# Attention and feed-forward in one kernel: the bias rows of the last eight groups stored in two steps, q, k and v loaded whole, bias read with fewer transfers

## Chip, cores and metric

One core of one Trainium2 chip. The metric is the device time of one execution in microseconds (us); three runs of the kernel before gave 684.4 us in the median (683.91 to 684.7).

## What is computed

Attention over q, k, v of shape (4 batches, 8 heads, 576 positions, 64), with an additive bias that a small network makes from the two positions, then a feed-forward layer over the 2304 tokens. Cut from the reference:

```python
scores = scale * np.matmul(q, k.transpose(0, 1, 3, 2))
pos = np.arange(S)
rel = (pos[:, None] - pos[None, :]).astype(np.float32)
psi_rel = np.log1p(np.abs(rel))
psi_i = np.log1p(np.maximum(pos[:, None].astype(np.float32), 1.0))
x = (psi_rel / psi_i)[..., None]
h = np.maximum(x @ w1 + b1, 0.0)
bias = h @ w2
scores = scores + bias.transpose(2, 0, 1)[None, :, :, :]
...
x = np.ascontiguousarray(attn_out.transpose(0, 2, 1, 3)).reshape(B * S, H * D)
h = x @ w_in
g = np.maximum(0.01 * h, h)
return (g @ w_out).astype(np.float32)
```

The bias depends on head and positions alone, so it is made once (8 x 576 x 576 numbers) and used for all four batches.

## The kernel before

**Bias generation.** The 576 query rows are made in 36 row groups of 16, in the order of the list GEN (line 35). A group has 16 rows by 8 heads, so it fills 128 partitions. Groups are counted here from 0 to 35 by their place in that order. For each, VectorE (DVE) and ScalarE (ACT) make the hidden layer (`gen_r`, line 115), TensorE (PE) contracts it (`gen_mm`, line 128), and ACT evicts the result into an SBUF buffer (`gen_ev`, line 139); the second part of the last three evictions is DVE's. SyncE (SP) then stores the group to one of five DRAM tensors (line 158): groups 2 to 9 make tensor 0, 10 to 17 tensor 1, 20 to 27 tensor 2, 28 to 35 tensor 3, and groups 0, 1, 18, 19 tensor M. The store also turns the relative layout into rows.

**Attention.** There are 16 units, a unit being one pair of heads in one batch; the pair changes every fourth unit. A unit has nine score tiles, in the order A0, B0, A1, B1, M, A2, B2, A3, B3 (A and B are the two heads, the number is the block of 128 queries, M holds the last 64 queries of both heads). `step(n)` (line 365) handles tile n = 9 u + i: q k^T on PE into one of two buffers `ps_s` (`qk_mm`), then on DVE the sum with the bias and the row minimum (`softmax_a`, line 277), the transposes of tile n-3 on PE, the product with v (`pv`, line 344), and the exponential on ACT. Tiles with number 0, 1, 2, 3 and M read the bias loaded from the tensor of that name. `load_bias` (line 171) loads a head pair from such a tensor: three transfers for a numbered one, two for M. Its calls during generation are in `gen_tick` (line 167); the later pairs are loaded during units 3, 7 and 11.

**Unit inputs.** `load_unit` (line 187) loads q and k of a unit twice, once to partitions 0 to 63 and once to 64 to 127, in four transfers; `load_v` (line 195) loads v in one transfer of 512 columns and two small ones (the last 64 keys, padded with zeros that DVE writes at the start). From unit 1 on, q and k are split into a rounded part (DVE, lines 207 and 212) and a rest (GpSimd, lines 219 and 222).

**Order.** All of this is written out by hand: each engine runs its instructions in the order of the code. SP issues all DMAs, in one queue, in that order. Each DMA is given one of eight semaphores in turn; before one is issued, the DMA that held the same semaphore eight places earlier must have landed (waits named DMAHW0 to DMAHW7 below). A load of bias also waits for the stores of its tensor. During unit 0 the code runs all of the generation first (line 37), then step 0. After the attention comes the feed-forward part, which the change doesn't touch.

Of the kernel before, what the change touches and what calls it, by code (L numbers as in the profile page):

```python
# [8 lines left out]
F32 = mybir.dt.float32  # L9
# [25 lines left out]
GEN = [16, 17] + list(range(16)) + [34, 35] + list(range(18, 26)) + list(range(33, 25, -1))  # L35
# [4 lines left out]


@with_exitstack
def attention_ffn(ctx: ExitStack, tc: tile.TileContext, qt, kt, vm, vt, wi, wo, cst, out):
    nc = tc.nc
    PS = bass.MemoryType.PSUM
    xp = ctx.enter_context(tc.tile_pool(name="xp", bufs=1))
# [16 lines left out]
    raw_b = [[ap.tile([128, c], F32, name=f"raw{c}{i}") for c in (2 * S, KW)] for i in range(2)]  # L63
    ident = ap.tile([128, 128], F32, name="ident")
    make_identity(nc, ident[:])
    vt_b = [ap.tile([128, 2, 64], F32, name=f"vt{i}") for i in range(3)]
    for t in vt_b:
        nc.vector.memset(t[0:64, 1, :], 0.0)
        nc.vector.memset(t[64:128, 0, :], 0.0)
# [4 lines left out]
    raw_0 = [gp.tile([128, c], F32, name=f"raw{c}") for c in (2 * S, KW)]  # L74
# [4 lines left out]
    e_b = [gp.tile([128, W], F32, name=f"e{i}")[:] for i in range(7)]  # L79
# [18 lines left out]
    gr, gps = {}, {}  # L98

    def gen_w(T):  # L100
        return max(S - 16 * T, 16 * T + 16)
# [2 lines left out]
    for T in GEN:  # L104
# [4 lines left out]
        for _ in range(4):  # L109
            e = min(cost, key=lambda c: load[c] + cost[c])  # L110
# [28 lines left out]
    def gen_ev(T):  # L139
        pt, o0 = gps.pop(T)  # L140
        R, F = 16 * T + 15, S - 16 * T
        e = e_b[GEN.index(T) % len(e_b)]
        nc.scalar.activation(out=e[:, R:W], in_=pt[:, o0:o0 + F], func=AF.Copy, scale=ips[:, T:T + 1])  # L143
        if GEN.index(T) < 33:
            nc.scalar.activation(out=e[:, 0:R], in_=pt[:, o0 + R:o0:-1], func=AF.Copy, scale=ips[:, T:T + 1])
        else:
            nc.vector.tensor_scalar(out=e[:, 0:R], in0=pt[:, o0 + R:o0:-1], scalar1=ips[:, T:T + 1], scalar2=None, op0=ALU.mult)
        if T < 16:
            c, r0 = str(T // 8), 16 * (T % 8)
        elif T < 18:  # L150
            c, r0 = "M", 16 * (T - 16)
        elif T < 34:
            c, r0 = str(2 + (T - 18) // 8), 16 * ((T - 18) % 8)
        else:
            c, r0 = "M", 32 + 16 * (T - 34)
        a = r0 * H * PIT + 1
        dst = scr[c][a:a + 16 * (H * PIT + 1)].rearrange("(i x) -> i x", i=16)[:, 0:H * PIT].rearrange("i (h p) -> i h p", h=H)[:, :, 0:W]
        nc.sync.dma_start(out=dst, in_=e)

    def gen_tick(g):  # L160
        if g + 1 < 36:
            gen_r(g + 1)
# [24 lines left out]
    def load_unit(u):  # L187
        hp, b = divmod(u, B)
        q_, k_ = raw_b[u % 2] if u else raw_0
# [3 lines left out]
        raw[u] = (q_, k_)  # L193

    def load_v(u):
        hp, b = divmod(u, B)
        v_ = ap.tile([128, 4, 128], F32, tag="v", name="v", bufs=3)
        nc.sync.dma_start(out=v_[:], in_=vm[hp, b])
        for h in range(2):
            nc.sync.dma_start(out=vt_b[u % 3][64 * h:64 * h + 64, h, :], in_=vt[hp, b, h])  # L200
        vv[u] = v_

    def split_hi(u, what):
        q_, k_ = raw[u]
        if what == "q":
            qs = qs_b[u % 2]
            nc.vector.tensor_copy(qs[:].rearrange("p (a c) -> p a c", a=2), q_[:].rearrange("p (a c) -> p a c", a=2)[:, :, 64:S])  # L207
            ks1 = ap.tile([128, KW], F32R, tag="ks1", name="ks1", bufs=2)
            ks2 = ap.tile([128, KW], F32R, tag="ks2", name="ks2", bufs=2)
            qk[u] = (qs, ks1, ks2)  # L210
        else:
            nc.vector.tensor_copy(qk[u][1][:], k_[:])

    def split_lo(u, what, a):
        q_, k_ = raw[u]
# [128 lines left out]
    def pv():  # L344
        _, u, g = pv_q.pop(0)
        hp, b = divmod(u, B)
        o, pt = outs.pop((u, g)), PT[:, g]
        if (u, g) == (HP * B - 1, 1):
            o = pstile("s")
        for jb in range(5):  # L350
            for h in range(2):
                if jb < 4:
                    l, r = vv[u][:, jb, 64 * h:64 * h + 64], pt[:, 2 * jb + h, :]
                else:
                    l, r = vt_b[u % 3][:, h, :], pt[:, 8, :]
# [233 lines left out]
    with tc.manual_schedule():  # L589
# [6 lines left out]
        for n in range(NTILE + LAG + 6):  # L596
            u, i = divmod(n, 9)
# [55 lines left out]
        pt = pv_out[0][3]  # L653
# [185 lines left out]
```

## Time and profile before

| | us |
|---|---|
| median of 3 runs | 684.4 |
| the profiled execution | 685.03 |
| its span, first to last instruction | 683.3 |
| PE busy | 675.2 |
| DVE busy | 492.1 |
| ACT busy | 407.9 |
| POOL busy | 205.8 |

The span is divided into bias generation (to about 49 us), unit 0 (to about 60 us), the other units (to about 302 us) and the feed-forward part. PE is busy in nearly all of it; DVE and ACT are busiest at the start. Engine names: PE TensorE, PEld its weight loads, DVE VectorE, ACT ScalarE, POOL GpSimd, SP SyncE with its DMA queue.

### The profile page before, as it was taken

What the parts mean: (1) busy time and instruction counts of PE and PEld (TensorE: products, weight loads), DVE (VectorE), ACT (ScalarE), POOL (GpSimd) and SP (SyncE); (2) the same over time, 40 slices, a digit from 0 to 9 for tenths busy, and PEclk for the clock granted to TensorE, in tenths of its full rate; (3) what the DMA queues carried; (4) which work ended last, traced back from release to release, by engine and by line L of the source; (5) the groups of instructions that cost most, each with busy time, mean ns of one, the idle gap of its engine ahead of it and who ended that gap; (6) DMA issues with size and microseconds to landing.
All of it is one profiled execution on the core that took longest, in us unless ns stands there. A gap on an engine that the chain in (4) does not pass through costs nothing.

```text
span 683.3 us, 11911 instructions
## 1 busy us (share of the span) xinstructions
PE 675.2 (99%) x4254; PEld 551.8 (81%) x4254; DVE 492.1 (72%) x1083; ACT 407.9 (60%) x883; POOL 205.8 (30%) x227
## 2 busy tenths in 40 slices
PE   9999999999999999999999999999999999999997
PEld 5436778887778777787889898898989898988986
DVE  8997789999999998589999868534343754343342
ACT  8987777888878888685555455333333543333332
POOL 0004445666666654420000503111114512111110
PEclk9999999999999999999999999999999999999999
DMA  9997679669955976135267336532333345332302
GB/s 213 350 324 201 194 219 248 175 199 269 282 166 164 307 226 197 55 114 202 94 200 244 141 94 230 195 115 108 107 108 108 122 173 196 141 109 108 108 1 92
DMA packets 39931, 117.85 MB, mean 172 GB/s; under 512 B 9024, under 2 KB 13760, under 8 KB 37440
## 3 DMA queue, kind: packets, MB, share of 16 engines
q1 hardware_dynamic: 39728, 116.96, 54.2%
q8 instruction: 33, 0.54, 0.3%
q14 instruction: 26, 0.21, 0.1%
q10 hardware_dynamic: 144, 0.13, 0.1%
HBM read 86.78 MB, written 30.29 MB: 171 GB/s over the span
## 4 chain that ended last, share of the span: by engine, by line
PE 91%; DVE 3%; ACT 2%; DMA 2%; issue 1%; POOL 0%; DVEq 0%; SPq 0%; POOLq 0%; ACTq 0%
PE ps_t L522 24%; PE ps_s L563 19%; PE ps_o L356 12%; PE ps_s L254 10%; PE ps_o L563 10%; PE ps_t L319 9%; DVE r L125 2%; PE ps_s L239 1%; PE ps_o L308 1%; PE ps_o L337 1%; DMA w1a<-w 1%; DMA bias<-scr 1%; PE ps_t L136 1%; PE ps_o L136 1%; ACT x L143 1%
## 5 line engine op out<-in xcount | busy, mean ns | idle before, releaser
L534 DVE TENSOR_TENSOR c<-ps_t,c 128x384 f32<-128x384 f32 x164 | 88.9, 555 | 130.5 <-PE ps_t L522 129.4
L541 ACT ACTIVATE g<-c 128x384 fp32r<-128x384 f32 x96 | 50.4, 525 | 181.1 <-DVE c L534 157.0
L563 PE MATMUL ps_s<-ws,g 128*128 128x512 f32 x576 | 148.3, 393 | 0.0
L563 PEld LDWEIGHTS ps_s<-ws,g 128*128 128x128 f32 x576 | 106.7, 188 | 16.9
L277 DVE CUSTOM_DVE_ANT_0 p<-ps_s,bias 128x576 f32<-128x576 f32 x128 | 95.4, 752 | 20.6 <-PE ps_s L254 18.1
L285 ACT ACTIVATE p<-p,mx 128x576 f32<-128x576 f32 x128 | 99.9, 780 | 9.0 <-DVE mx L277 6.7
L522 PE MATMUL ps_t<-xo,w1c 128*128 128x384 f32 x504 | 99.8, 336 | 0.8 <-DVE c L534 0.6
L472 POOL TENSOR_TENSOR ws<-y,ws 128x512 fp32r<-128x512 f32 x32 | 42.7, 1334 | 184.2 <-PE ps_t L522 147.4
L335 ACT COPY PT<-ps_t 128x512 f32<-128x512 f32 x128 | 73.8, 577 | 40.0 <-PE ps_t L319 40.0
L522 PEld LDWEIGHTS ps_t<-xo,w1c 128*128 128x128 f32 x504 | 89.3, 188 | 8.8 <-DVE c L534 2.3
L254 PE MATMUL ps_s<-ks,qs 128*128 128x288 f32 x480 | 93.7, 317 | 0.0
L522 PE MATMUL ps_t<-xo,w1a 128*128 128x384 f32 x474 | 93.2, 335 | 0.0
L522 PEld LDWEIGHTS ps_t<-xo,w1a 128*128 128x128 f32 x474 | 84.4, 188 | 5.9
L254 PEld LDWEIGHTS ps_s<-ks,qs 128*128 128x128 f32 x480 | 67.6, 189 | 13.3 <-issue 4.8
L319 PE MATMUL ps_t<-ident,p 128*128 128x128 f32 x512 | 77.5, 274 | 0.0
L563 PE MATMUL ps_o<-ws,g 128*128 128x512 f32 x288 | 74.0, 393 | 0.0
L546 DVE TENSOR_TENSOR g<-gf,g 128x384 fp32r<-128x384 f32 x96 | 61.1, 637 | 14.5 <-ACT gf L542 14.4
L319 PEld LDWEIGHTS ps_t<-ident,p 128*128 128x128 f32 x512 | 61.0, 140 | 9.1 <-issue 8.2
L356 PE MATMUL ps_o<-PT,v 128*64 128x288 f32 x496 | 67.0, 412 | 0.0
L219 POOL TENSOR_TENSOR qs<-raw,qs 64x512 fp32r<-64x512 f32 x30 | 37.8, 1279 | 75.0 <-DVE qs L207 73.4
L563 PEld LDWEIGHTS ps_o<-ws,g 128*128 128x128 f32 x288 | 53.4, 188 | 8.5
L356 PEld LDWEIGHTS ps_o<-PT,v 128*64 128x64 f32 x496 | 32.9, 136 | 23.6 <-issue 2.7
(131 smaller groups left out, 913.7 us busy)
## 6 DMA issues: line engine op xcount, KB each, us to landing
w1a<-w SPq DMA_DIRECT2D x10, 1792.0 KB, 7.7
w1c<-w SPq DMA_DIRECT2D x9, 1792.0 KB, 7.5
raw<-kt SPq DMA_DIRECT2D x32, 304.0 KB, 6.0
raw<-qt SPq DMA_DIRECT2D x32, 288.0 KB, 4.5
w<-w1a SPq DMA_DIRECT2D x20, 448.0 KB, 5.5
raw<-wi SPq DMA_DIRECT2D x16, 512.0 KB, 3.8
raw<-wo SPq DMA_DIRECT2D x16, 512.0 KB, 4.7
scr<-x SPq DMA_DIRECT2D x21, 295.5 KB, 5.2
```

The lines of the kernel that those rows point to most:

```text
L254: nc.tensor.matmul(s_[:, S0 + HS * hh:S0 + HS * hh + HS], qs[:, c0:c0 + 128], ks[:, k0 + HS * hh:k0 + HS * hh + HS], start=(j == 0), stop= ...
L277: nc.vector.tensor_tensor_reduce(out=p, in0=s_[:, S0:S0 + S], in1=bt, scale=-0.125, scalar=3.4e38, op0=ALU.add, op1=ALU.min, accum_out=i)
L285: nc.scalar.activation(out=p, in_=p, func=AF.Exp, bias=i, scale=-1.0, accum_out=sm)
L319: nc.tensor.transpose(t0[:, 128 * jb:128 * jb + 128], p[:, p0 + 128 * jb:p0 + 128 * jb + 128], ident[:])
L335: nc.scalar.copy(out=PT[:, g, 0:8, c].rearrange("p (j h) c -> p j h c", h=2)[:, :, h, :], in_=t0[:].rearrange("p (j c) -> p j c", j=4))
L356: nc.tensor.matmul(o[64 * h:64 * h + 64, 0:HS], l, r, start=(jb == 0), stop=(jb == 4))
L472: eng.tensor_sub(t[:, 1], y2[c % MF][:], t[:, 0].bitcast(F32))
L522: nc.tensor.matmul(o, w[:, a, PROD[j], c], x[:, b, k, :], start=(n == 0), stop=(n == 5))
L534: nc.vector.tensor_add(a if c == src else c_new(g, c), bank[g, j], a)
L541: nc.scalar.activation(out=t[:, 0], in_=h, func=AF.Prelu, alpha=0.01)
L546: nc.vector.tensor_sub(t[:, 1], gf.pop((g, c))[:], t[:, 0].bitcast(F32))
L563: nc.tensor.matmul(o, t[:, a, c], w[:, b], start=(m == 0 and n == 0), stop=(m == NG - 1 and n == 5))
```

## The change

- Groups 28 to 35 (tensor 3) are stored in two steps. During generation only the rows of the first two heads are stored, in one transfer per head (16 rows of 591 numbers). The whole rows of all eight heads are stored during unit 0, one group in each of the steps 5 to 12.
- The buffers of the evictions are taken two places further on, so that those of the last eight groups lie in the tiles `x1`, which stay free until unit 4.
- The bias of tensor 2 is loaded at tick 34 of the generation instead of tick 37. Loads of a numbered tensor are two transfers (128 x 2 x 512 and 128 x 2 x 64), that of M is one: 128 rows, taken from DRAM with the two heads as the outer dimension and 64 rows within each.
- q and k of a unit, both copies, come in one transfer of 128 x 2368 numbers, and v with its padded last block in one of 128 x 640. The host lays them out so. The six memsets of DVE are gone.

The core of the diff:

```diff
@@ gen_ev
-        e = e_b[GEN.index(T) % len(e_b)]
+        e = e_b[(GEN.index(T) + 2) % len(e_b)]
...
-        nc.sync.dma_start(out=dst, in_=e)
+        if GEN.index(T) < 36 - LATE:
+            nc.sync.dma_start(out=dst, in_=e)
+        else:
+            for h in range(2):
+                nc.sync.dma_start(out=dst[:, h], in_=e[h::H])
+            late.append((dst, e))
@@ gen_tick
-        for c in {16: "0", 24: "1", 27: "M", 37: "23"}.get(g, ()):
+        for c in {16: "0", 24: "1", 27: "M", 34: "2", 37: "3"}.get(g, ()):
@@ load_bias
-            nc.sync.dma_start(out=t[0:64, :], in_=rows[:, 2 * hp, :])
-            nc.sync.dma_start(out=t[64:128, :], in_=rows[:, 2 * hp + 1, :])
+            nc.sync.dma_start(out=t[:], in_=rows[:, 2 * hp:2 * hp + 2, :].rearrange("i h p -> h i p"))
...
-            nc.sync.dma_start(out=t[:, 0, :], in_=rows[:, 2 * hp, :])
-            nc.sync.dma_start(out=t[:, 1, 64:S], in_=rows[:, 2 * hp + 1, 0:512])
-            nc.sync.dma_start(out=t[:, 1, 0:64], in_=rows[:, 2 * hp + 1, 512:S])
+            f, two = t[:].rearrange("p h c -> p (h c)"), rows[:, 2 * hp:2 * hp + 2, :]
+            main = bass.AP(f.tensor, f.offset, [f.ap[0], [640, 2], [1, 512]])
+            nc.sync.dma_start(out=main, in_=two[:, :, 0:512])
+            nc.sync.dma_start(out=f[:, 512:640].rearrange("p (h c) -> p h c", h=2), in_=two[:, :, 512:S])
@@ load_unit
-        for t, src in ((q_, qt), (k_, kt)):
-            for p in (0, 64):
-                nc.sync.dma_start(out=t[p:p + 64], in_=src[hp, b])
+        nc.sync.dma_start(out=t[:], in_=qk_in[hp, b])
@@ load_v
-        v_ = ap.tile([128, 4, 128], F32, tag="v", name="v", bufs=3)
-        nc.sync.dma_start(out=v_[:], in_=vm[hp, b])
-        for h in range(2):
-            nc.sync.dma_start(out=vt_b[u % 3][64 * h:64 * h + 64, h, :], in_=vt[hp, b, h])
+        v_ = ap.tile([128, 5, 128], F32, tag="v", name="v", bufs=3)
+        nc.sync.dma_start(out=v_[:], in_=v_in[hp, b])
@@ step
+            if 5 <= n < 5 + LATE:
+                dst, e = late[n - 5]
+                nc.sync.dma_start(out=dst, in_=e)
```

SP's queue before, from the load of M to the loads of tensors 2 and 3 (scr_81 is tensor 2, scr_82 tensor 3; x_69 and x_70 hold evicted groups; a DMA row's shape is its destination's):

```order
L176 DMA biasM<-scrM 64x576 [waits DMAHW1_49]
L177 DMA biasM<-scrM 64x576 [waits DMAHW2_49]
L158 DMA scr_81<-x_69 16x8x591 [waits DMAHW3_49,Activation_49]
L158 DMA scr_82<-x_69 16x8x591 [waits DMAHW4_49,Activation_49]
...
L158 DMA scr_82<-x_70 16x8x591 [waits DMAHW3_49,DVE_49]
L180 DMA bias<-scr_81 128x576 [waits DMAHW4_49]
L181 DMA bias<-scr_81 128x512 [waits DMAHW5_49]
L182 DMA bias<-scr_81 128x64 [waits DMAHW6_49]
L180 DMA bias<-scr_82 128x576 [waits DMAHW3_49,DMAHW2_49,DMAHW7_49,DMAHW1_49,DMAHW0_49]
```

The same place in the change, from the load of M to the second DMA of group 31, which is the ninth behind it:

```order
L178 DMA biasM<-scrM 128x1x576 [waits DMAHW5_49]
L156 DMA scr_81<-x_69 16x8x591 [waits DMAHW6_49,Activation_49]
L159 DMA scr_82<-x_69 16x591 [waits DMAHW7_49,Activation_49]
L159 DMA scr_82<-x_69 16x591 [waits DMAHW0_49]
L159 DMA scr_82<-x_69 16x591 [waits DMAHW1_49,Activation_49]
L159 DMA scr_82<-x_69 16x591 [waits DMAHW2_49]
L159 DMA scr_82<-x_70 16x591 [waits DMAHW3_49,Activation_49]
L159 DMA scr_82<-x_70 16x591 [waits DMAHW4_49]
L159 DMA scr_82<-x_70 16x591 [waits DMAHW5_49,Activation_49]
L159 DMA scr_82<-x_70 16x591 [waits DMAHW6_49]
```

The load of M is one row where there were two, and the first DMA of group 31 waits for the semaphore that this load holds (DMAHW5). Behind these rows, to the late stores, the queue reads in the change:

```order
L159 DMA scr_82<-x_70 16x591 [waits DMAHW1_49,DVE_49]
L159 DMA scr_82<-x_70 16x591 [waits DMAHW2_49]
L183 DMA bias<-scr_81 128x2x512 [waits DMAHW3_49]
L184 DMA bias<-scr_81 128x2x64 [waits DMAHW4_49]
L159 DMA scr_82<-x_70 16x591 [waits DMAHW5_49,DVE_49]
...
L183 DMA bias<-scr_82 128x2x512 [waits DMAHW5_49,DMAHW6_49,DMAHW2_49,DMAHW7_49,DMAHW1_49,DMAHW0_49]
L184 DMA bias<-scr_82 128x2x64
L192 DMA raw_84<-qk_in 128x2368 [waits DMAHW3_49]
L367 DMA scr_82<-x_69 16x8x591 [waits DMAHW4_49,DMAHW2_49,DMAHW1_49]
```

The loads from tensor 2 stand four stores further ahead than before (behind group 33 instead of 35), those from tensor 3 still stand behind the last store of that tensor, and the whole-row stores stand behind the q and k of unit 2.

## Rows read from the trace of the kernel before

**Rows 1.** The page's first part: busy time, share of the span, instructions.

```profile
PE 675.2 (99%) x4254; PEld 551.8 (81%) x4254; DVE 492.1 (72%) x1083; ACT 407.9 (60%) x883; POOL 205.8 (30%) x227
```

**Rows 2.** Chain that ended last, 0 to 66 us: start us, us, what.

```profile
50.91 4.77 DMA bias<-scr
...
55.81 0.76 DVE p L277
...
56.63 0.76 PE ps_s L248 x4
...
60.90 2.58 PE ps_o L356 x20
```

**Rows 3.** Windows of 2 us: PE, PEld, DVE, ACT, POOL busy, PEclk, DMA share, GB/s.

```profile
6.00:8.00 2.00, 2.00 (x28) 1.11 (x21) 1.86 (x5) 1.51 (x4) 0.00 (x0) 1.00 1.01 237
22.00:24.00 2.00, 2.00 (x19) 0.89 (x15) 2.00 (x8) 2.00 (x7) 0.00 (x0) 1.00 1.04 377
54.00:56.00 2.00, 1.53 (x11) 0.83 (x9) 0.23 (x2) 1.27 (x4) 0.00 (x0) 1.00 0.60 214
56.00:58.00 2.00, 1.37 (x9) 0.83 (x10) 1.57 (x6) 1.39 (x4) 0.98 (x4) 1.00 0.89 269
```

**Rows 4.** Timeline of DVE, 55 to 80 us: start us, us, what, [idle before <-releaser].

```profile
55.81 0.76 DVE L277 CUSTOM_DVE_ANT_0 p<-ps_s,bias 128x576 f32<-128x576 f32 x1 [1.77 <-DMA bias<-scr]
...
58.03 0.76 DVE L277 CUSTOM_DVE_ANT_0 p<-ps_s,bias 128x576 f32<-128x576 f32 x1 [0.43 <-PE ps_t L319]
...
59.33 0.69 DVE L309 COPY PT<-ps_o 128x512 f32<-128x512 f32 x1
...
65.30 0.68 DVE L207 CAST qs<-raw 128x1024 fp32r<-128x1024 f32 x1
```

**Rows 5.** Timeline of PE, 46 to 64 us.

```profile
55.26 0.27 PE L337 MATMUL ps_o<-ident,p 128*128 128x128 f32 x1
56.63 0.76 PE L248 MATMUL ps_s<-raw,raw 64*128 64x288 f32 x4 [1.10 <-DVE mx L277]
...
59.57 0.78 PE L254 MATMUL ps_s<-ks,qs 128*128 128x288 f32 x4
...
60.83 2.16 PE L356 MATMUL ps_o<-PT,v 128*64 128x288 f32 x16
```

**Rows 6.** Timeline of SP's DMA issues, 0 to 62 us.

```profile
13.52 1.23 SPq L158 DMA_DIRECT2D scrM<-e  x2
...
40.96 0.52 SPq L158 DMA_DIRECT2D scr<-x  x1
41.54 0.64 SPq L176 DMA_DIRECT2D biasM<-scrM  x1
...
43.37 7.49 SPq L158 DMA_DIRECT2D scr<-x  x9
50.91 0.70 SPq L180 DMA_DIRECT2D bias<-scr  x1
...
55.17 0.32 SPq L180 DMA_DIRECT2D bias<-scr  x1
55.53 0.43 SPq L181 DMA_DIRECT2D bias<-scr  x1
```

**Rows 7.** Timeline, ends of the evictions of groups 0, 26, 31 and 35.

```profile
7.24 0.48 ACT L145 ACTIVATE e<-ps_t,cs 128x271 f32<-128x271 f32 x1
...
37.82 0.69 ACT L145 ACTIVATE x<-ps_t,cs 128x399 f32<-128x399 f32 x1
...
43.43 0.84 ACT L145 ACTIVATE x<-ps_t,cs 128x495 f32<-128x495 f32 x1
...
48.11 0.67 DVE L147 TENSOR_SCALAR x<-ps_t,cs 128x431 f32<-128x431 f32 x1 [0.23 <-ACT x L143]
```

**Rows 8.** Stores `scr<-x` to 62 us: count, issue ns min/median/max, first and last start.

```profile
L158 SPq DMA_DIRECT2D scr<-x x21: 523/764/1173, 19.5 to 50.0; - x21
```

**Rows 9.** Tile `bias` to 62 us: from issue to landing, its twelve transfers.

```profile
DMA to landing us min/median/max: 2.7/4.4/5.9
```

**Rows 10.** DMA issues: count, KB of each, median us from issue to landing.

```profile
out<-x SPq DMA_DIRECT2D x1, 128.0 KB, 1.9
```

More of the change, by code (lines that the diff above doesn't have):

```diff
@@ L27 @@
 RAWS = 3
+LATE = 8
 PRE = 3
@@ L42, in attention_ffn @@
 @with_exitstack
-def attention_ffn(ctx: ExitStack, tc: tile.TileContext, qt, kt, vm, vt, wi, wo, cst, out):
+def attention_ffn(ctx: ExitStack, tc: tile.TileContext, qk_in, v_in, wi, wo, cst, out):
     nc = tc.nc
@@ L61, in pstile @@
         return ps.tile(shape, F32, tag=tag, name="ps_" + tag)
-    raw_b = [[ap.tile([128, c], F32, name=f"raw{c}{i}") for c in (2 * S, KW)] for i in range(2)]
+    raw_b = [ap.tile([128, 2 * S + KW], F32, name=f"raw{i}") for i in range(2)]
     ident = ap.tile([128, 128], F32, name="ident")
     make_identity(nc, ident[:])
[L66 to L69, printed above, removed]
     qs_b = [ap.tile([128, 1024], F32R, name=f"qs{i}") for i in range(2)]
     PT = ap.tile([128, 2, 10, HS], F32, name="PT")
-    raw_0 = [gp.tile([128, c], F32, name=f"raw{c}") for c in (2 * S, KW)]
+    raw_0 = gp.tile([128, 2 * S + KW], F32, name="raw")
     cs = gp.tile([128, S + 214], F32, name="cs")
@@ L96, in gen_setup @@
         nc.gpsimd.tensor_scalar(out=w2d, in0=w2d, scalar1=8.0, scalar2=None, op0=ALU.mult)
-    gr, gps = {}, {}
+    gr, gps, late = {}, {}, []
     def gen_w(T):
@@ L188, in load_unit @@
         hp, b = divmod(u, B)
-        q_, k_ = raw_b[u % 2] if u else raw_0
-        for t, src in ((q_, qt), (k_, kt)):
-            for p in (0, 64):
-                nc.sync.dma_start(out=t[p:p + 64], in_=src[hp, b])
-        raw[u] = (q_, k_)
+        t = raw_b[u % 2] if u else raw_0
+        nc.sync.dma_start(out=t[:], in_=qk_in[hp, b])
+        raw[u] = (t[:, 0:2 * S], t[:, 2 * S:2 * S + KW])
     def load_v(u):
         hp, b = divmod(u, B)
-        v_ = ap.tile([128, 4, 128], F32, tag="v", name="v", bufs=3)
-        nc.sync.dma_start(out=v_[:], in_=vm[hp, b])
-        for h in range(2):
-            nc.sync.dma_start(out=vt_b[u % 3][64 * h:64 * h + 64, h, :], in_=vt[hp, b, h])
+        v_ = ap.tile([128, 5, 128], F32, tag="v", name="v", bufs=3)
+        nc.sync.dma_start(out=v_[:], in_=v_in[hp, b])
         vv[u] = v_
@@ L206, in split_hi @@
             qs = qs_b[u % 2]
-            nc.vector.tensor_copy(qs[:].rearrange("p (a c) -> p a c", a=2), q_[:].rearrange("p (a c) -> p a c", a=2)[:, :, 64:S])
+            nc.vector.tensor_copy(qs[:].rearrange("p (a c) -> p a c", a=2), q_.rearrange("p (a c) -> p a c", a=2)[:, :, 64:S])
             ks1 = ap.tile([128, KW], F32R, tag="ks1", name="ks1", bufs=2)
@@ L211, in split_hi @@
         else:
-            nc.vector.tensor_copy(qk[u][1][:], k_[:])
+            nc.vector.tensor_copy(qk[u][1][:], k_)
     def split_lo(u, what, a):
@@ L351, in pv @@
             for h in range(2):
[L352 to L355, printed above, removed]
+                l, r = vv[u][:, jb, 64 * h:64 * h + 64], pt[:, 2 * jb + h if jb < 4 else 8, :]
                 nc.tensor.matmul(o[64 * h:64 * h + 64, 0:HS], l, r, start=(jb == 0), stop=(jb == 4))
@@ L810 @@
     kd = np.concatenate([kd[0::2], kd[1::2, :, :, 512:], kd[1::2]], -1)
+    qkd = np.concatenate([qd.reshape(HP, B, D, 2 * S), kd], -1)
+    qkd = np.concatenate([qkd, qkd], 2)
     vd = v.transpose(1, 0, 2, 3).reshape(HP, 2, B, S, D).transpose(0, 2, 3, 1, 4).reshape(HP, B, S, 2 * D)
     vm = vd[:, :, :512].reshape(HP, B, 4, 128, 128).transpose(0, 1, 3, 2, 4)
-    vt = vd[:, :, 512:].reshape(HP, B, 64, 2, D).transpose(0, 1, 3, 2, 4)
+    vt = np.zeros((HP, B, 128, 1, 128), np.float32)
+    vt[:, :, :64, 0, :D] = vd[:, :, 512:, :D]
+    vt[:, :, 64:, 0, D:] = vd[:, :, 512:, D:]
+    vm = np.concatenate([vm, vt], 3)
     wi = inputs["moe_w_in"].reshape(KC, 128, MF, 128).transpose(2, 1, 0, 3).reshape(DFF, DM)
@@ L827 @@
     cst = np.concatenate([wb, np.repeat(psi, HID, axis=0), ipsi, np.repeat(lt, 128, axis=0)], axis=1)
-    arrays = {"qt": qd, "kt": kd, "vm": vm, "vt": vt, "wi": wi, "wo": wo, "cst": cst}
+    arrays = {"qk_in": qkd, "v_in": vm, "wi": wi, "wo": wo, "cst": cst}
     arrays = {n: np.ascontiguousarray(a) for n, a in arrays.items()}
```

## The prediction

> **What bounds the kernel now.** I read the busy shares first. PE is busy in 99% of the span [rows 1], so an edit counts only if it lets PE start or go on earlier, or makes it wait. Then the chain that ended last: past 60.90 us it is PE's own work for nearly all of the rest, with one entry ahead of it that is no engine's, the DMA `bias<-scr` from 50.91 us for 4.77 us [rows 2]. That is the load of bias tensor 2, which tile A2 of unit 0 needs. It is issued only when the last stores have been [rows 6]. In the timelines DVE stands idle 1.77 us for it, ahead of A2 at 55.81 [rows 4], and PE, which cannot fill the next score buffer before A2 is read, 1.10 us at 56.63 [rows 5]. The windows agree: in 54 to 58 us PE is busy 1.53 + 1.37 of 4 us, so it loses 1.10 [rows 3]. This is all that the change can give back: DVE's other 0.67 us lie beside PE's work, which ends at 55.53 (55.26 + 0.27) [rows 5].
>
> Before that stage PE counts as busy, but is paced by the generation: DVE and ACT are busy 2.00 of 2.00 us in the middle of it while the DMA engines too are full (share 1.04 at 377 GB/s) [rows 3]. DMA is late, not the engines: group 26 was evicted at 38.51 (37.82 + 0.69) [rows 7] and stored from 40.96 [rows 6], 2.45 us behind.
>
> **The change, part by part.**
>
> *q, k and v in two loads.* Two units are loaded at the start, 2 x 1472 KB or 3.0 MB. In halves of the partitions they run at 237 GB/s with the engines full (share 1.01); the stores, which touch all 128 partitions, run at 377 [rows 3]. 3.0 MB take 12.7 us at the first rate; the change's 3.1 MB take 8.2 at the second. The first store could be issued when its group is evicted, at 7.72 (7.24 + 0.48) [rows 7], instead of 13.52 [rows 6]. Nobody waits for that store, and DVE and ACT stay full, so it is worth nothing by itself; the cover is the 2.00 of 2.00 us of both. It removes most of the 2.45 us by which SP is late at group 26. I keep 0.6 us of lag, with 0 and 2.45 as the ends: once the loads are done sooner, the DMA engines need some 0.86 us per group (0.303 MB at the 350 GB/s between both rows) and the generation makes one in some 1.2 us ((48.78 - 7.72) / 35) [rows 7], but the first groups still queue behind the loads. In later units the same loads are off the path: the cast of unit 2's q at 65.30 waits for no DMA [rows 4]. The six memsets lie ahead of the first constant and cost nothing either way.
>
> *Two heads of the last eight groups.* 8 x 295.5 KB become 16 x 36.9 KB: 1.8 MB less ahead of the bias loads, 4.8 us at 377 GB/s. Against it stand eight more issues; one takes 0.523 us at least when unhindered [rows 8], I use 0.55 with the gap. The two of a group (1.1 us) fit between two groups (1.2 us).
>
> *Tensor 2 loaded from tick 34, tensor 3 as before.* The loads of 2 pass four stores in the queue. Without any hindrance they would be issued soon after 48.5 and land ahead of 54.04, when DVE would be ready for A2 (55.81 - 1.77), and all of the 1.10 us would come back. Tensor 3 follows the last small store. A3 would then be wanted at 56.93 (58.03 - 1.10) [rows 4].
>
> *M in one load.* Here the trace of before has no like. In all its transfers both sides count 16 rows or more in their outer dimension; in the new one the source's outer dimension is the two heads. If the work is dealt out to the 16 engines by that dimension, only two of them carry it. Bounds: on 16 engines 288 KB at 377 GB/s take 0.8 us. On two, an engine moves 377 / 16 / 1.04 = 22.7 GB/s [rows 3], so 64 rows of 2304 B take 6.5 us. The nearest rows, all with 16 or more on both sides, fill the 16 engines, but none has a small outer count; I take 6.5 us, because a transfer has to be cut along some dimension and two is all that this one offers there. [...] By the other end of the bounds the sum would be 1.10 us less instead of 1.5 more.
>
> *What queues behind it.* SP lets eight DMAs be under way. The eighth behind the load of M is the first small store of group 31, and in the new order it waits for M's semaphore. Step by step:
> - M is issued at 39.1 (38.51 and one store issue) plus 0.6 of lag: 39.7. A transfer of 128 KB lands 1.9 us after its issue [rows 10], of which 0.35 are its own bytes; with 1.55 + 6.5, and 0.8 for a store that is still in the two engines, M lands at 48.5. Tile M itself reads it at about 52, in time.
> - Group 31 was evicted at 44.27 (43.43 + 0.84) [rows 7], but its store goes out at 48.5. From there ten small stores at 0.55 and two loads of tensor 2 at 0.45 follow back to back: 6.4 us, to 54.9. The loads of tensor 2, behind six of the stores, are issued at 51.8 and 52.3 and land 2.7 us after issue at the least [rows 9], at about 55: A2 starts some 0.8 us earlier than now.
> - The last small store, issued at 54.35, lands 1.9 us later: 56.3. Only then tensor 3 is loaded: its second transfer is issued 0.45 later, lands 2.7 after that at the least [rows 9], and 0.6 more for the 224 KB by which its first transfer is larger than before: 60.0. At the median of 4.4 us it would be 61.
> - A3 starts at 60.1 instead of 58.03. PE goes on with unit 1 0.82 us after the start of the tile that it waits for (56.63 - 55.81) [rows 4, 5]: 60.95, against 59.57. The product with v needs the copy at 59.33 [rows 4], which stands behind A3 and moves with it, 2.0 us after its start, to 62.1; PE reaches it then at 62.3, against 60.83. So 1.4 to 1.5 us are lost; I take 1.5.
>
> *Whole rows during unit 0.* 2.4 MB more, 6.7 us of the engines, behind q and k of unit 2. Those land near 63, ahead of the cast at 65.30 + 1.5. Unit 3's loads are asked for in unit 1, when this is over. Cost 0; uncovered, a late cast would cost up to 1 us.
>
> **Sum.** 0 + 0 (wait for tensor 2 gone) + 1.5 (new wait for tensor 3). The profiled execution of 685.03 us becomes 686.5. That execution was 0.6 us longer than the median of 684.4, so by the median I expect **685.9 us**. With no lag at M the loss is 0.9, with the lag of before 3.3. A measurement of this kernel can tell about 0.2%, 1.4 us, from no change: from 683.0 to 685.8 counts as the same.
>
> **The rivals.**
>
> *M on all 16 engines (not slower).* Then M lands at about 42, the stores go out as groups come, the last at 51.2, tensor 3 lands at about 56.4 to 57.2, when A3 wants it, and the 1.10 us of PE come back: 683.3 by the median. For it: every transfer in the profile fills the engines. Against it: none has two as its outer count. The point that decides is whether M lands ahead of 44.3, when group 31 wants its slot. Chance 0.22.
>
> *SP itself is held at M.* An issue takes 0.523 us unhindered but up to 1.173 where the engines are full [rows 8], so the queue pushes back. If 64 rows for one engine stop SP until most of them are gone, the stores of groups 27 to 30 queue up too: seven issues, 3.9 us, less the 2 or so that the engines get ahead. The loss is 3 us, 687.4. Chance 0.13.
>
> *Faster than measurement hides.* If PE could use all of DVE's 1.77 us, because its work up to 55.53 moves up too, the time would be 682.6. Against it: PE is busy there behind DVE, which runs A0 to M without a gap. Chance 0.10, most of it for what I overlook.
>
> *The loads are no faster for being whole.* Then SP is as late at M as before, and the loss goes towards 3.3; this is the upper part of my own case.
>
> **How the numbers follow.** My case has 0.55. Its bounds, 0.9 to 3.3 us with the weight near 1.5, lie on both sides of 1.4, so 0.33 of it is slower and 0.22 the same. Slower: 0.33 + 0.13 = 0.46. Same: 0.22 + 0.22 = 0.44. Faster: 0.10. The range reaches from the rival with 16 engines, 683.2, to the held SP and lag, 687.6; it leaves out the faster case and the far end. My case alone runs from 685.3 to 687.0.
>
> **What would show it.** In the profile after: the load of M lands 8 us or more after its issue; the first small store of group 31 is issued near 48 and not near 44.5; A2 waits at most 1 us, and A3 instead waits some 2 to 3 us for `bias<-scr`; PE's wait moves from ahead of the tile behind A2 to the first tile of unit 1. The rate at the start is near 377 GB/s. I am wrong if M lands in less than 5 us, if A3 waits for nothing, or if a wait appears in units 1 to 3 for q, k or the late stores.

## The result and the profile after

The changed kernel takes **688.85 us** in the median of six runs (687.55 to 689.49), against 684.55 for the kernel before on the same chip (683.8 to 685.49): a ratio of **1.0057** with a 95% interval from 1.0041 to 1.0073, or some 3.9 us more (the two medians as they stand differ by 4.3). The profiled execution took 689.49 us, the longest of the six, with a span of 687.7, against 685.03 and 683.3. The prediction, 685.9 with a range to 687.6, had the sign right and a loss that is too small: 1.5 us.

First the DMA issues of SP in the changed kernel (start us, us of a run of issues, line, destination <- source, count). Lines of the changed kernel stand about two lower than before: L156 stores whole rows, L159 the small stores of two heads, L178 loads M, L183 and L184 are the two transfers of a numbered bias, L367 the late whole rows.

```profile
7.98 2.00 SPq L156 DMA_DIRECT2D scrM<-e  x2
...
39.29 0.62 SPq L178 DMA_DIRECT2D biasM<-scrM  x1
40.02 0.55 SPq L156 DMA_DIRECT2D scr<-x  x1
40.93 12.41 SPq L159 DMA_DIRECT2D scr<-x  x12
53.39 0.57 SPq L183 DMA_DIRECT2D bias<-scr  x1
54.01 0.47 SPq L184 DMA_DIRECT2D bias<-scr  x1
54.58 2.37 SPq L159 DMA_DIRECT2D scr<-x  x4
58.36 0.36 SPq L183 DMA_DIRECT2D bias<-scr  x1
58.77 0.46 SPq L184 DMA_DIRECT2D bias<-scr  x1
59.29 0.46 SPq L192 DMA_DIRECT2D raw<-qk_in  x1
62.28 3.63 SPq L367 DMA_DIRECT2D scr<-x  x4
```

Bias tensor 2, issued from 50.91 before although it stood behind all stores [rows 6], is issued at 53.39 although it now stands ahead of four of them; tensor 3 is issued at 58.36 where it was at 55.17. The first store goes out at 7.98 instead of 13.52 [rows 6]. What SP waited for between 36 and 64 us (engine and line, what it waited for, us in total, times, longest):

```profile
SPq L159 <- DMA biasM<-scrM: 3.5, 1, 3.5
SPq L367 <- DMA bias<-scr: 2.5, 1, 2.5
SPq L183 <- DMA scr<-x: 0.9, 1, 0.9
```

So one small store stood 3.5 us behind the load of M. The chain that ended last gives the times (start us, us, what):

```profile
39.29 9.94 DMA biasM<-scrM
...
49.69 1.78 DMA scr<-x
...
54.01 3.62 DMA bias<-scr
...
57.80 0.76 DVE p L275
...
58.61 1.33 PE ps_s L246 x4
...
65.61 2.58 PE ps_o L351 x20
```

M landed at 49.23, 9.94 us after its issue, and is the longest entry of the chain in this stretch; before, the chain had no entry for it. The product with v that follows the wait starts at 65.61 instead of 60.90 [rows 2]: 4.71 us later, the whole loss of the span (4.4) and a little that is won back. The windows show what else happened (stretch, its length, busy us of PE, PEld, DVE, ACT, POOL, granted clock of PE, DMA share, GB/s):

```profile
6.00:8.00 2.00, 2.00 (x27) 1.15 (x21) 1.88 (x5) 1.26 (x4) 0.00 (x0) 1.00 0.94 343
...
47.00:48.00 1.00, 1.00 (x8) 0.30 (x4) 1.00 (x2) 0.35 (x2) 0.00 (x0) 1.00 0.13 51
...
54.00:56.00 2.00, 1.65 (x12) 0.86 (x10) 0.17 (x1) 1.39 (x4) 0.00 (x0) 1.00 0.70 159
56.00:58.00 2.00, 0.00 (x0) 0.00 (x0) 0.20 (x1) 0.00 (x0) 0.00 (x0) 1.00 0.68 228
58.00:60.00 2.00, 1.39 (x5) 0.63 (x6) 1.48 (x6) 1.41 (x4) 0.99 (x4) 0.52 0.31 32
60.00:62.00 2.00, 2.00 (x10) 1.67 (x12) 0.00 (x0) 1.29 (x3) 2.00 (x2) 0.50 1.09 386
62.00:64.00 2.00, 2.00 (x9) 1.24 (x10) 1.57 (x5) 0.75 (x2) 0.69 (x1) 0.50 0.98 417
64.00:66.00 2.00, 2.00 (x14) 1.70 (x15) 1.83 (x6) 1.62 (x6) 0.00 (x0) 0.78 0.90 310
```

In 6 to 8 us, while q, k and v are loaded, 343 GB/s flow where it was 237 [rows 3]. In 47 to 48 us SP issues nothing, because it waits for M; the DMA share is 0.13, which is two engines of 16 (0.125), at 51 GB/s, and the trace's DMA packets in that stretch are two at a time, of 2304 bytes, which is one row of M. In 56 to 58 us PE does nothing, where it had been busy 1.37 of 2 us [rows 3]. And from 58 us its granted clock is 0.50, until some time in 64 to 66; in the kernel before it is 1.00 in all these stretches. DVE's tiles A2 and A3 in its timeline (the bracket is the idle time before, and what ended it):

```profile
57.80 0.76 DVE L275 CUSTOM_DVE_ANT_0 p<-ps_s,bias 128x576 f32<-128x576 f32 x1 [3.63 <-DMA bias<-scr]
...
62.39 0.76 DVE L275 CUSTOM_DVE_ANT_0 p<-ps_s,bias 128x576 f32<-128x576 f32 x1 [2.88 <-DMA bias<-scr]
```

A2 waits 3.63 us for its bias instead of 1.77, and A3, which waited 0.43 us for a transpose [rows 4], waits 2.88 us for bias too. PE's timeline:

```profile
58.61 1.33 PE L246 MATMUL ps_s<-raw 64*128 64x288 f32 x4 [2.96 <-DVE mx L275]
...
63.80 1.27 PE L252 MATMUL ps_s<-ks,qs 128*128 128x288 f32 x4
```

PE's wait grew from 1.10 to 2.96 us [rows 5]. The same four products then take 1.33 us and not 0.76, and the first tile of unit 1 starts at 63.80 instead of 59.57 [rows 5]. Of the 4.71 us this gives two parts. A3 lets PE go on 0.82 us after its start, at 63.21 at the earliest: 3.64 us later than 59.57 without any loss of clock. The other 1.07 us are an estimate of what the half clock costs; the third experiment tests it.

### The profile page after: what moved, and what is told of

The parts are those of the page before. It is cut to its first block, busy times and chain, and to the rows that moved or that the text cites. A ratio compares the mean times of both kernels' runs of the same rounds, so it can differ in the third digit from the quotient of the medians.

```text
span 687.7 us, 11696 instructions
## 1 busy us (share of the span) xinstructions
PE 677.6 (99%) x4254; PEld 553.1 (80%) x4254; DVE 491.7 (71%) x1077; ACT 408.1 (59%) x883; POOL 206.1 (30%) x227
## 4 chain that ended last, share of the span: by engine, by line
PE 88%; ACT 4%; DVE 3%; DMA 3%; issue 1%; SPq 0%; POOL 0%; DVEq 0%; POOLq 0%; ACTq 0%
PE ps_t L520 24%; PE ps_s L561 19%; PE ps_o L351 12%; PE ps_s L252 10%; PE ps_o L561 10%; PE ps_t L317 9%; DMA biasM<-scrM 1%; PE ps_s L237 1%; PE ps_o L306 1%; PE ps_o L335 1%; ACT r L120 1%; ACT x L140 1%; DVE xo L509 1%; DVE c L532 1%; ACT e L140 1%
## 5 line engine op out<-in xcount | busy, mean ns | idle before, releaser
L351 PE MATMUL ps_o<-PT,v 128*64 128x288 f32 x620 | 82.0, 411 | 0.0
L351 PEld LDWEIGHTS ps_o<-PT,v 128*64 128x64 f32 x620 | 41.8, 136 | 29.7 <-issue 2.9
## 6 DMA issues: line engine op xcount, KB each, us to landing
scr<-x SPq DMA_DIRECT2D x24, 295.5 KB, 4.6
```

## The experiments

"Ratio" always compares a kernel's executions with those of the kernel before on the same chip, with its 95% interval. It is not the quotient of the two medians, which differs from it by up to 0.0017. 0.001 is 0.68 us. Times with a start are from the profiled execution of each kernel.

**M in two loads again.** The changed kernel with

```diff
-            nc.sync.dma_start(out=t[:], in_=rows[:, 2 * hp:2 * hp + 2, :].rearrange("i h p -> h i p"))
+            nc.sync.dma_start(out=t[0:64, :], in_=rows[:, 2 * hp, :])
+            nc.sync.dma_start(out=t[64:128, :], in_=rows[:, 2 * hp + 1, :])
```

> The changed kernel with the load of M in two transfers again (64 rows on both sides), all else as changed. Theory (the load of M in one transfer runs on two engines, lands 9.9 us after its issue and holds back the small stores): M lands 4 to 6 us after issue, the small stores of group 31 go out near 44.5 us instead of 49.7, tile A2 waits for nothing, A3 for at most 0.5 us, PE does not fall to half clock, and the time is about 1 us below the kernel before, 683.0 to 684.0. Rival (sixteen small stores and the wait for the last of them are the cost, wherever M lands): A2 or A3 still waits 2 us or more and the time stays above 686.

Ratio 1.0017 (1.0004 to 1.003), 685.5 us. The two loads land 4.8 and 5.4 us after issue, tensor 2 is issued at 50.64 instead of 53.39, and the clock stays at 1.00. The timelines of DVE and PE, A3 and the first tile of unit 1:

```profile
59.56 0.76 DVE L276 CUSTOM_DVE_ANT_0 p<-ps_s,bias 128x576 f32<-128x576 f32 x1 [2.99 <-DMA bias<-scr]
```

```profile
60.38 0.80 PE L253 MATMUL ps_s<-ks,qs 128*128 128x288 f32 x4 [1.51 <-DVE mx L276]
```

The one transfer of M carries 0.0040 of the loss, 2.7 us of 3.9. But the 1.10 us do not come back: A2 waits only 0.70 us, and A3 takes the wait over, 2.99 us of DVE and 1.51 of PE. Some cost lies in other parts of the change.

**M in one load in the kernel before.** The reverse edit, alone, in the kernel before:

```diff
-            nc.sync.dma_start(out=t[0:64, :], in_=rows[:, 2 * hp, :])
-            nc.sync.dma_start(out=t[64:128, :], in_=rows[:, 2 * hp + 1, :])
+            nc.sync.dma_start(out=t[:], in_=rows[:, 2 * hp:2 * hp + 2, :].rearrange("i h p -> h i p"))
```

> The kernel before with only the load of M put into one transfer. Theory: M lands 9 us or more after its issue at 41.5 us, the whole-row stores queue behind it in two engines, and the bias of tensor 2 comes some 3 us later than before: time 687 to 690. Rival (the new order of SP's queue is needed for the loss): not slower than 685.5.

Ratio 1.0103 (1.0073 to 1.0133), 692.14 us. That is more than the 687 to 690 us expected. A2 starts at 58.02 after 4.00 us without work on DVE, and PE stands 3.34 us; the windows show the share of two engines and the half clock again:

```profile
56.00:58.00 2.00, 0.00 (x0) 0.00 (x0) 0.00 (x0) 0.00 (x0) 0.00 (x0) 0.93 0.13 51
58.00:60.00 2.00, 1.16 (x4) 0.51 (x4) 1.76 (x6) 1.18 (x3) 0.76 (x3) 0.50 0.82 228
```

So the one load costs at least as much without the rest of the change (0.0103) as with it (0.0040). Its mechanism does not need the small stores: here it holds a whole store for 2.1 us. In 56 to 58 us M has long landed: the nine stores behind it, of which one waited for it, were all issued by 51.59 (41.48 + 10.11). What still moves at the share of two engines was issued behind it, the stores and the loads of tensor 2, since SP issues nothing between 53.88 (53.36 + 0.52) and 57.34. Unit 0 is not the whole loss of this trace: the product with v starts 4.69 us later than before (65.52, 60.83 [rows 5]), and the span is 6.5 us longer (689.8, 683.3). Where the rest lies was not split.

**PE kept busy in the wait.** The changed kernel, with 13 products of the identity with itself ahead of the scores of step 7, so that the wait is filled:

```diff
+        if n == 7:
+            wt = pstile("t")
+            for _ in range(13):
+                nc.tensor.matmul(wt[:, 0:128], ident[:], ident[:], start=True, stop=True)
```

> The changed kernel with 13 products of the identity on PE (128 columns each, their result unused) ahead of the score tile A3 of unit 0, where PE stands idle 2.96 us. Nothing else moves; the waits for bias stay. Theory (the granted clock of 0.5 from 58.6 to 64.8 us, behind that idle time, is a cost of its own of about 1 us): the clock stays at 1.0, A2 and A3 wait as long as in the changed kernel, and the time is 0.7 to 1.4 us below it. Rival (the slow stretch is hidden behind the wait for A3): the same time as the changed kernel within 0.4 us.

Ratio 1.0046 (1.003 to 1.0062), 687.65 us. The products fill 3.12 us from 55.43, the clock stays at 1.00 everywhere, and the first tile of unit 1 takes 0.79 us instead of 1.27. Against the changed kernel the ratio is 0.0011 lower, 0.75 us; the intervals overlap, so the time alone does not show the gain. The clock does: its mean over an execution is 0.999 or 1.00 in all nine here, and 0.994 to 0.998 in all six of the changed kernel. In the traces, of one execution each, the product with v starts 1.81 us earlier (63.73 for 65.54), of which 0.75 are A3 itself (61.64 for 62.39), so 1.06 are the clock. That agrees with the 1.07 above.

**M asked for earlier.** The changed kernel with the load of M at tick 22:

```diff
-        for c in {16: "0", 24: "1", 27: "M", 34: "2", 37: "3"}.get(g, ()):
+        for c in {16: "0", 22: "M", 24: "1", 34: "2", 37: "3"}.get(g, ()):
```

> The changed kernel with the load of M in one transfer as changed, but issued at tick 22 of the generation instead of 27. Theory (what costs is that eight places behind it stands a small store that is ready at 44.3 us; a slow transfer with time behind it costs nothing): M still takes 9 us or more to land, but has landed by about 44 us, the stores of group 31 go out within 1.5 us of their eviction, and the time is 683.0 to 685.0. Rival (two engines that are held for 6 us cost their time wherever that is): 686.5 or more.

Ratio 1.0077 (1.0055 to 1.01), 690.2 us: a miss, slower still. SP's waits, 30 to 64 us:

```profile
SPq L178 <- DMA scrM<-e: 3.6, 1, 3.6
SPq L156 <- DMA biasM<-scrM: 3.2, 1, 3.2
```

M's load waits for the stores of M's own tensor, groups 18 and 19, and SP with it, 3.6 us. It is issued at 36.64, only 2.65 us sooner, and then holds a store for 3.2 us all the same. Tensor 2 goes out at 54.96, A2 starts at 59.38. The earlier place moved the wait ahead of more stores. That a slow load with time behind it costs nothing is therefore not tested here.

**Whole rows, M in two loads.** The first experiment with the last eight groups stored whole and once. Kept are the merged loads, tick 34 and two transfers of a numbered bias.

```diff
-LATE = 8
+LATE = 0
```

> The changed kernel with M in two transfers, and with the last eight groups stored as whole rows during generation, as before (no late stores); q, k and v stay merged, tensor 2 is loaded at tick 34, numbered bias in two transfers. Theory (sixteen small stores at 0.6 to 0.7 us of SP each cost as much time of the queue as they save of the DMA engines, since the merged loads have already emptied these): A2 waits for at most 0.7 us, A3 less than the 2.99 us that it waits with small stores, and the time is at or below that of M in two transfers alone (685.5 beside 683.9 for the kernel before), by 0.5 to 2 us. Rival (the DMA engines are too full for whole rows): A2 waits 1.5 us or more and the time is no better than 685.5.

Ratio 1.0019 (1.0004 to 1.0034), 685.56 us: no different from 1.0017 with the small stores. Neither the theory nor the rival fits in full. The small stores save bytes and yet buy no time that shows. A2 now waits for nothing (53.75), and A3 waits longer instead of less, 3.87 us:

```profile
59.34 0.76 DVE L276 CUSTOM_DVE_ANT_0 p<-ps_s,bias 128x576 f32<-128x576 f32 x1 [3.87 <-DMA bias<-scr]
```

PE waits 2.06 us, and in this trace too the clock is 0.50 behind that wait. It was not so in every execution; the last section comes back to it.

**Three transfers for a numbered bias.** The first experiment with the three transfers of the kernel before, whose first one is the first head alone:

```diff
-            nc.sync.dma_start(out=main, in_=two[:, :, 0:512])
-            nc.sync.dma_start(out=f[:, 512:640].rearrange("p (h c) -> p h c", h=2), in_=two[:, :, 512:S])
+            nc.sync.dma_start(out=t[:, 0, :], in_=rows[:, 2 * hp, :])
+            nc.sync.dma_start(out=t[:, 1, 64:S], in_=rows[:, 2 * hp + 1, 0:512])
+            nc.sync.dma_start(out=t[:, 1, 0:64], in_=rows[:, 2 * hp + 1, 512:S])
```

> The changed kernel with M in two transfers and the numbered bias tensors in three, as before; small stores and merged loads stay. Theory (in two transfers tile A3 waits for both heads, 576 KB, where before it waited for the first transfer of 288 KB alone): the wait of A3 falls from 2.99 us by about 1 us, and the time by 0.8 to 1.2 us against M in two transfers alone. Rival (what A3 waits for is the round trip behind the last small store): the wait falls by less than 0.4 us.

Ratio 1.0011 (0.9999 to 1.0024). A3 starts 2.89 us after tensor 3's first issue (58.12, 55.23), where with two transfers it took 4.00 (59.56, 55.56). The difference of 1.1 us shows in A3's start. The wait itself falls by only 0.41 us, from 2.99 to 2.58, since the tiles ahead come earlier too; in the time nothing is resolved (0.0006, about 0.4 us, of the 0.8 to 1.2 us expected).

**The loads of q, k and v alone.** All else as before: whole rows, M in two loads, numbered bias in three, both last tensors at tick 37. The shift of the buffers stays. To the edits of the two experiments above comes

```diff
-        for c in {16: "0", 24: "1", 27: "M", 34: "2", 37: "3"}.get(g, ()):
+        for c in {16: "0", 24: "1", 27: "M", 37: "23"}.get(g, ()):
```

> The kernel before with only q, k and v merged (and the eviction buffers two places further on); bias loads, their places and the stores as before. Theory (merged loads empty the DMA engines some 4 us earlier, which the stores and the load of tensor 2 inherit): A2 waits less than the 1.77 us of before, between 0 and 1, and the time is 0.3 to 1.1 us below the kernel before. Rival (the order of the queue, and not the full engines, makes the wait): A2 waits as long as before and the time is the same within 0.3 us.

Ratio 0.9989 (0.9976 to 1.0002), 683.97 us. Timeline of DVE:

```profile
53.90 0.76 DVE L275 CUSTOM_DVE_ANT_0 p<-ps_s,bias 128x576 f32<-128x576 f32 x1 [0.21 <-PE ps_t L317]
...
55.92 0.76 DVE L275 CUSTOM_DVE_ANT_0 p<-ps_s,bias 128x576 f32<-128x576 f32 x1 [0.21 <-PE ps_s L246]
```

Neither A2 nor A3 waits for bias any more, PE has no wait between the stages, and the product with v starts at 59.18 instead of 60.83 [rows 5]: in the trace the 1.10 us and 0.55 more are won back with none of the other parts. In the time the gain is 0.75 us by the ratio, with 1.0 inside the interval: not resolved.

**The same with tensor 2 at tick 34.** That kernel, with the tick table of the change:

```diff
-        for c in {16: "0", 24: "1", 27: "M", 37: "23"}.get(g, ()):
+        for c in {16: "0", 24: "1", 27: "M", 34: "2", 37: "3"}.get(g, ()):
```

> The kernel before with q, k and v merged and tensor 2 loaded at tick 34; M in two transfers, numbered bias in three, whole-row stores. Theory: this holds all that helps and none of what hurts; A2 waits for nothing or next to it, A3 at most 0.5 us, PE loses none of its 1.10 us, and the time is 0.8 to 1.3 us below the kernel before. Rival (the two transfers of a store and a load that pass each other cost as much as they give): the same as merged loads alone.

Ratio 1.0001 (0.999 to 1.0013). Its SP issues (L182 to L184 are the three transfers):

```profile
47.48 0.68 SPq L182 DMA_DIRECT2D bias<-scr  x1
48.20 0.83 SPq L183 DMA_DIRECT2D bias<-scr  x1
49.09 0.44 SPq L184 DMA_DIRECT2D bias<-scr  x1
49.63 1.16 SPq L156 DMA_DIRECT2D scr<-x  x2
54.63 0.33 SPq L182 DMA_DIRECT2D bias<-scr  x1
```

Tensor 2 passes two stores and goes out 1.74 us earlier than at tick 37 (49.22), when A2 wants nothing more. The last two stores follow it, and tensor 3, which waits for them, goes out at 54.63 instead of 52.87. A3 moves from 55.92 to 57.59 and PE waits 0.35 us. Moving tensor 2 ahead is paid by tensor 3.

**M in one load, rows outermost.** The changed kernel with the `rearrange` taken out of the load of M:

```diff
-            nc.sync.dma_start(out=t[:], in_=rows[:, 2 * hp:2 * hp + 2, :].rearrange("i h p -> h i p"))
+            nc.sync.dma_start(out=t[:], in_=rows[:, 2 * hp:2 * hp + 2, :])
```

> The changed kernel with M still in one transfer of the same 128 rows of 576 numbers, but taken from DRAM with the 64 rows as the outer dimension and the two heads within (the bias of M then lies in other partitions than the scores: the last 64 queries of each batch get wrong bias; nothing else differs). Theory (a transfer is dealt out to the engines by its outer dimension, and two heads outermost leave two engines): M lands 4 to 6 us after issue instead of 9.9, DMA share and rate do not fall to 0.13 and 51 GB/s in 47 to 48 us, and the time is that of M in two transfers, 685 to 686. Rival (one transfer of two heads' rows is slow whatever the order): M lands 8 us or more after issue and the time is 688 or more.

Ratio 1.0006 (0.9998 to 1.0015), 684.62 us: 0.0051, or 3.5 us, less than the changed kernel, with the same bytes in the same single transfer at the same place in the queue. Tile biasM:

```profile
DMA to landing us min/median/max: 5.6/5.6/5.6
```

5.6 us instead of 9.94, and none of SP's waits from 36 to 64 us is for M. A2 waits 0.55 us and A3 2.94, as with M in two loads. One sign that was named does not separate:

```profile
47.00:48.00 1.00, 1.00 (x8) 0.30 (x4) 1.00 (x2) 0.35 (x2) 0.00 (x0) 1.00 0.15 46
```

The share is as low here, but M has landed at 44.9, and small stores go out one by one. The landing of M and the wait behind it separate. They settle the first cause: not that M is one transfer, but that the two heads are its outermost count.

**The loads alone, without the shift of the buffers.** The kernel of 0.9989 with

```diff
-        e = e_b[(GEN.index(T) + 2) % len(e_b)]
+        e = e_b[GEN.index(T) % len(e_b)]
```

> The kernel before with q, k and v merged and nothing else (eviction buffers where they were): a second measurement of that part. Theory: A2 waits for no DMA, unit 1 starts some 1.1 to 1.6 us earlier than before, 0.3 to 1.4 us below the kernel before. Rival (the shifted buffers made the gain): the time of the kernel before within 0.2 us.

Ratio 1.0000 (0.9991 to 1.0008). PE's timeline:

```profile
55.75 0.76 PE L246 MATMUL ps_s<-raw 64*128 64x288 f32 x4 [0.21 <-DVE mx L275]
```

PE's wait at A2 is 0.21 us instead of 1.10, and the product with v starts at 59.94, 0.89 us earlier than before, yet the time shows nothing: the gain of 0.3 us or more that was expected did not come. The traced execution of the kernel before was itself 0.6 us longer than its median, which may be part of the 0.89. Whether the merged loads are worth some tenths of a us or none stays open.

**Small stores, both tensors at tick 37.** The kernel with three transfers and small stores (1.0011), with

```diff
-        for c in {16: "0", 24: "1", 27: "M", 34: "2", 37: "3"}.get(g, ()):
+        for c in {16: "0", 24: "1", 27: "M", 37: "23"}.get(g, ()):
```

> The changed kernel with M in two transfers, numbered bias in three and tensor 2 loaded at tick 37 again, behind the last stores: what is left of the change is the merged loads and the small stores. Theory (at tick 34 the load of tensor 2 passes the last stores and delays tensor 3): A3 waits at least 0.8 us less for its bias than with tick 34, A2 waits at most 1 us, time 0.5 to 1 us below that with tick 34 (685.4 beside 684.4 for the kernel before). Rival (the small stores themselves hold tensor 3 back): the same time within 0.3 us.

Ratio 1.0022 (0.9997 to 1.0047). Its SP issues:

```profile
41.98 0.55 SPq L156 DMA_DIRECT2D scr<-x  x1
42.63 10.61 SPq L159 DMA_DIRECT2D scr<-x  x16
53.29 0.57 SPq L182 DMA_DIRECT2D bias<-scr  x1
```

Sixteen small stores take 10.61 us, though M is not in their way: 0.66 each with one gap of half a us, 0.63 without it. In 45 to 48 and 50 to 54 us the DMA share is 0.18 to 0.22, so it is the issues that set the pace, not the bytes. Tensor 2 goes out at 53.29, where in the kernel of 0.9989, the same but with whole stores, it goes at 49.22. A2 waits 2.37 us, against the 1 us at most that was expected, and PE 1.71. Between these two kernels the small stores cost 0.0033, 2.3 us, with intervals that just overlap.

**M in one load, whole rows.** The kernel of 0.9989 with the load of M as in the change:

```diff
-            nc.sync.dma_start(out=t[0:64, :], in_=rows[:, 2 * hp, :])
-            nc.sync.dma_start(out=t[64:128, :], in_=rows[:, 2 * hp + 1, :])
+            nc.sync.dma_start(out=t[:], in_=rows[:, 2 * hp:2 * hp + 2, :].rearrange("i h p -> h i p"))
```

> The kernel before with q, k and v merged, and M in one transfer with the two heads outermost as in the change; whole-row stores, bias in three transfers at the old places. Theory (M on two engines holds back what queues behind it, whole rows more than small stores, since each has eight rows for each engine): M lands 9 us or more after issue, A2 waits 2.5 us or more, the granted clock falls behind it, 688 to 692. Rival (without the small stores SP has places enough to pass M): below 686.

Ratio 1.0036 (1.0022 to 1.005), 0.0047 or 3.2 us over the same kernel with two loads. M holds a store 1.2 us, nine stores take 10.47 us instead of 7.77, A2 starts at 56.38 instead of 53.90, and PE stands 2.13 us. The clock stays at 1.00 in this trace, but the traced execution (685.36 us) is shorter than the median (686.92).

The parts beside each other:

| kernel | ratio | interval |
|---|---|---|
| merged q, k, v loads | 1.0000 | 0.9991 to 1.0008 |
| + buffers shifted by two | 0.9989 | 0.9976 to 1.0002 |
| + tensor 2 at tick 34 | 1.0001 | 0.999 to 1.0013 |
| + bias in two transfers | 1.0019 | 1.0004 to 1.0034 |
| + small stores | 1.0017 | 1.0004 to 1.003 |
| + M in one load, heads outermost: the change | 1.0057 | 1.0041 to 1.0073 |
| the change with M rows outermost | 1.0006 | 0.9998 to 1.0015 |

The step to the change is clear: its interval lies apart from those of the row above it and of the row below it. The steps of tick 34 (+0.8 us) and of two transfers (+1.2 us) have the sign that the traces show at A3, but the intervals overlap each time. No version is faster than the kernel before by more than its interval.

## Why the prediction was right or wrong

In short: the path was right, from M on two engines over the store that waits for it to A3, and its length was not. What failed is the term of 1.5 us, the new wait for tensor 3, where the traces show 4.71 at the same place. The steps on the way to it (M's landing, the small stores, the two loads) were each sized too short, which put A3 at 60.1 where it came at 62.39; and the half clock, some 1 us, had no term at all.

*What bounds the stage: right.* The loss arises where the prediction put it, in the bias that unit 0 waits for; the kernel of the loads alone shows that the 1.10 us could be had. In that trace PE got 1.65 us, so the 1.10 was not quite all that there was; where the other 0.55 come from is not shown.

*Merged loads, worth nothing by themselves: not refuted by the time* (0.9989 and 1.0000), *but wrong in the traces.* The prediction gave the end of A2's wait to the loads of tensor 2 moved ahead. With merged loads alone A2 waits for no bias, and PE for 0 or 0.21 us instead of 1.10: SP is less late, and tensor 2 goes out at 49.22 or 50.17 instead of 50.91. The rate in 6 to 8 us rose from 237 to 343 GB/s, less than the 377 taken. M was issued at 39.29, with less lag than the 0.6 us assumed (39.7).

*M on two engines: right in mechanism, and decided against the rival with 16.* The row of 0.13 at 51 GB/s is two engines with 25.5 GB/s each, where 22.7 was estimated. That the two heads leave two engines was the author's estimate; the trace agrees, with its share of 0.13 and its packets two at a time. With 64 rows outermost the loss that M brings is gone (1.0006 for 1.0057). M landed 9.94 us after its issue instead of 8.8, at 49.23 instead of 48.5. The rival in which SP itself is held at the issue is out: the issue took 0.62 us, and the wait of 3.5 us is the semaphore of a store behind it. The rival with 16 engines was wrong on its time as well: with 64 rows of M outermost or with M in two loads the ratios are 1.0006 and 1.0017, where its 683.3 would be 0.9984, because then A3 waits.

*Tensor 2 0.8 us earlier: wrong, and this is where the sum first fails.* A2 came at 57.80, where 55.0 was forecast: 2.8 us later. The trace splits it. M landed 0.73 late, and the store that waited was issued 0.46 us after that and not at once. The six small stores took 0.61 each (49.69 to 53.34) instead of 0.55, 0.35 more. That makes nearly all of the 1.6 us by which the load went out at 53.39 instead of 51.8. The gap in the 0.55 was too small: 0.523 [rows 8] is the issue alone, and the kernel before shows the step from one issue to the next, with whole stores that start at 43.37, 44.02, 44.66 and 45.32, 0.65 apart. Then the second transfer followed 0.62 behind the first instead of 0.45, and landed in 3.62 us and not in 2.7. The prediction took the least of the twelve landings of before, though the first of the two transfers had become larger, and allowed 0.6 us for that at tensor 3 only.

*Small stores "fit between two groups": wrong.* Two of them take 1.26 us where the queue runs without a gap, and a group comes every 1.2, so a queue that is late once stays late. That they save 1.8 MB does not help, since here the issue and not the bytes sets when the queue is through: 1.0017 with them, 1.0019 without.

*Tensor 3 behind the last small store: right in mechanism, too early by 2.06 us* (58.36 instead of 56.3): 1.6 us are the delay of tensor 2's load carried on, and the rest is the two loads and four stores behind it, which again took more than 0.45 and 0.55 us each. Its landing was right within 0.3 us (4.03 from issue to A3, 3.8 forecast). What the prediction did not separate is that three transfers let A3 start with its own head. In two pairs of kernels the time from the issue to A3 is 2.9 to 3.0 us with three (58.12 - 55.23 and 57.59 - 54.63) and 4.0 to 4.1 with two (59.56 - 55.56 and 59.34 - 55.20).

*What is late next: half.* A3 waits 2.88 us, as forecast. But the wait ahead of the tile behind A2 did not go: it grew to 2.96 us, and this set off a term that the prediction did not have.

*The clock: missing.* The granted clock fell to 0.50 behind PE's wait of 2.96 us, and the prediction has no term for it. Of the 3.2 us between the forecast 62.3 and the 65.54 at which PE reached the product with v, 2.3 are A3 (62.39 for 60.1), and the 0.9 that are left are about the 1.07 found for the half clock above.

*Late whole rows at no cost: right.* In the change PE waits for nothing from 66 to 300 us, and the cast of unit 2's q starts at 70.00, 4.70 us later than before [rows 4], just as much as the work of PE ahead of it.

## What to carry to other kernels

Before two loads are made into one, look at the outermost count of the source: with two there, two of 16 engines carried 288 KB (share 0.13) and it landed in 9.94 us, with 64 in 5.6, and in the change the cost came not at the reader, which had time, but at a store eight places behind. In a queue that issues in order, price each added issue against the interval at which work reaches the queue, and read for every load moved ahead what waits for the stores that it passes. When a load is merged, ask whether its first reader needed only the first part.

## What the runs showed that was not expected

- PE's granted clock fell to 0.50 behind waits of PE of 2.96 us (the change, where it stayed there for 6.8 us), 4.67, 3.34, 2.06 and also 1.71 us, and did not fall behind waits of 1.10, 1.46, 1.51, and once 2.13 us. The length of the wait alone does not tell it; what else does was not tried. In the change the traces put its cost at 1.07 us; the 0.75 us between the ratios agrees, but is not resolved.
- Executions of one kernel differ in it. Of the twelve with whole rows and M in two loads, eight had a mean granted clock of 0.999 or 1.00 and took 684.5 to 685.6 us; four, the traced one among them, had 0.997 or 0.998 and took 687.0 to 688.0. With M in one load and whole rows it is three (685.0 to 686.0) and four (686.9 to 687.8). All of M in two loads and of rows outermost had 0.999 or 1.00. How much of these 2 us is the clock itself and how much a longer wait in the same execution is not separated, but a median depends on how many executions lost the clock.
- A small store is no cheaper to issue. Stores of 36.9 KB followed each other 0.63 us apart where nothing held them, and stores of 295.5 KB 0.64 to 0.66 (43.37, 44.02, 44.66 and 45.32 in the kernel before): an eighth of the bytes, the same time in the queue.
- A trace gain of 0.89 us at the end of unit 0 left no gain in the time of the whole (ratio 1.0000).
